# Two more units' outputs brought to features by TensorE, ScalarE for a first step, and a new written order

## The chip, the cores and the metric

The kernel runs on one core of one Trainium2 chip. The time is device microseconds of one execution; before, it is the median of three runs. A profiled execution gives a trace: for each engine (TensorE or PE, VectorE or DVE, ScalarE or ACT, GpSimd or POOL, and SyncE or SP, which issues DMAs) each instruction with its start and duration.

## The reference

A gated linear attention, one state matrix per batch and head, followed by a gated MLP. q, k, v and alpha are float32; the three weights are float64, which the kernel reads as pairs of 32-bit words.

```python
for t in range(S):                                  # B, H, S, D = 4, 8, 768, 48
    state = alpha[:, :, t, :, None] * state + einsum('bhd,bhe->bhde', k[:, :, t], v[:, :, t])
    y[:, :, t] = einsum('bhd,bhde->bhe', q[:, :, t], state)
x = y.transpose(0, 2, 1, 3).reshape(B * S, H * D)   # 3072 tokens, 384 features
g = x @ w_gate                                      # 384 -> 1536
return (g * sigmoid(g) * (x @ w_val)) @ w_out       # 1536 -> 384
```

## The kernel before, in words

**Attention.** The 768 steps of a batch are cut into four units of 192 steps, so there are 16 units, u = 0 to 15. Per unit: alpha, k and q are loaded (words La, Lk, Lq of the written order) and turned so that channels lie on partitions. For units 0 to 3 TensorE turns them (L394): a copy first spreads the rows (pa, pk, pq, L382), then T transposes them into PSUM, and ea, ek, cq copy them out (L798). For the later units VectorE transposes (tr, tk, tq, L374). Two scans on VectorE build the decay products (G, L439, and f, L448; z is a small memset behind f). mk multiplies k by them (L824 or L827), q does it for q (L465 or L467), and qc copies a part of that. k's rows are needed too: by TensorE's transposes (K, L492, copied out by kc, L496/L497) for units 0 to 3, by VectorE's (kr, L508) for the others. S are the scores on TensorE (L533), ma the causal mask on VectorE (L567). B (L557; Bw for units 0 to 3) are the states' updates, ad (L581 to L590) adds them up, de (L596) decays the state into the next unit, V loads the values (L413) and vc copies some of them. Y are the unit's outputs (L612 to L629), yh and yl split them into a high and a low part (L643, L647).

**To features.** The MLP wants the outputs with features on partitions, in the tile xT. For units 0 and 1 TensorE does it with selecting matrices (R, two matmuls a word, L669), and x copies the result out of PSUM (L673). For the other units SP issues ten DMAs a unit (xr, L686).

**MLP.** 3072 tokens are eight blocks of 384; d_ff is twelve slices f of 128. A step s is a block and a slice. Per step: product g (nine matmuls, high and low parts, L702), silu on ScalarE (sl, L710), product v (L702), their product h on VectorE (L714), its high part hh on ScalarE (L718) and low part hl on POOL or VectorE (L723), and nine matmuls o of the output (L734), summed over f in PSUM. Steps 0 to 6 are block 0 with f 0 to 6, steps 7 to 13 block 1 with the same, steps 14 to 18 block 0 with f 7 to 11, steps 19 to 23 block 1 with them; from step 24 on whole blocks follow. Each of the products g and v has one PSUM bank, so the next g waits for sl, the next v for h. ot copies a finished block out (L746), os stores it (L751).

**Weights.** 36 pieces in 20 groups: w0 to w2 and w19 hold one piece, the others two (in the order g0, v0, then g, v of slice f and o of slice f-1). wl loads a group's words (L277, L280), three steps v0, v1, v2 cut a float32 out of two words (L148, L151, L154, VectorE), a makes the high part (L321) and p the low part (L325). A group's words lie where the next group's result will lie. A range check of all weights (wr loads again, wc checks, L296 and L297, ScalarE) and of alpha (Lc, ck) runs in the later part; a flag at the end decides whether a general path runs instead, which never runs here.

**Order.** The program is written as one string, ORDER, of 1520 words engine:name@banks. Each engine runs its own words in that sequence (t TensorE, v VectorE, s ScalarE, g POOL, y SP); between engines only semaphores hold things back. The setting-up (memsets, ident, sel) stands outside the string, and the framework places it between the words. Before, the string began like this for TensorE, up to product v12, and for VectorE, up to h0:

```
t: Ta0 Ta1 Tq0 Tk0 Tk1 Tq1 S0 K0.0 K0.2 K0.1 Ta2 Bw0 K1.2 K1.1 K1.0 S1 Ta3 Y0 Bw1 Tk2 R0.2 Y1 Tq2 R0.1 K2.1 R0.0 K2.0
   K2.2 Tk3 R1.1 R1.2 R1.0 S2 Bw2 Tq3 Y2 g0 K3.1 v0 g1 S3 K3.2 K3.0 v1 o0 Bw3 g2 v2 Y3 g3 v3 o1 g4 v4 g5 o2 o3 v5 o4 g6
   v6 g7 v7 o5 g8 o6 v8 g9 v9 g10 o7 o8 v10 g11 o9 v11 g12 v12
v: w0v0 w0v1 w0v2 w1v0 w1v1 w1v2 G0 w1p f0 q0 mk0 G1 f1 ma0.2 w2v0 w2v1 w2v2 ma0.0 ma0.1 w3v0 w3v1 w3v2 de1 G2 f2 yl0.0
   ma1.0 ma1.2 yl0.1 ma1.1 mk2 w2p w4v0 w5v0 w5v1 w6v0 w4v1 w4v2 yl1.1 x0.0 yl1.0 de2 w6v1 w6v2 G3 ma2.2 mk3 ma2.1 ma2.0
   w7v0 w7v1 w7v2 de3 f3 yl2.0 yl2.1 h0
y: La0 wl0 wl1 Lq1 La1 Lq0 Lk0 V1 Lk1 La2 Lk2 V0 Lq2 La3 wl2 wl3 Lk3 wl4 ... wl17 xr2 wl18 V4 V5 xr3 La4 La5 Lq4 ...
```

Of the kernel before, what the change touches and what calls it, by code (L numbers as in the profile page):

```python
# [43 lines left out]
y:La0 y:wl0 y:wl1 y:Lq1 y:La1 y:Lq0 y:Lk0 s:pa0 y:V1 t:Ta0@01 v:w0v0 v:w0v1 s:ea0 v:w0v2 v:w1v0 v:w1v1 s:w0a v:w1v2  # L44
v:G0 s:w1a y:Lk1 s:pa1 y:La2 s:pq0 t:Ta1@01 v:w1p y:Lk2 t:Tq0@23 v:f0 g:z0 s:pk0 y:V0 t:Tk0@45 s:pq1 v:q0 g:pk1 g:w0p
v:mk0 t:Tk1@23 s:ea1 y:Lq2 s:ek1 t:Tq1@45 v:G1 y:La3 t:S0@01 y:wl2 s:qc0 y:wl3 t:K0.0@2 s:pa2 t:K0.2@3 v:f1 g:z1
s:kc0.0 t:K0.1@6 y:Lk3 s:vc0 y:wl4 s:kc0.1 y:wl5 v:ma0.2 g:mk1 s:kc0.2 t:Ta2@26 s:pa3 y:wl6 t:Bw0@1 v:w2v0 s:cq1
v:w2v1 y:wl7 v:w2v2 g:q1 t:K1.2@3 v:ma0.0 s:ad0.1 t:K1.1@4 t:K1.0@5 v:ma0.1 s:kc1.2 y:wl8 s:kc1.1 v:w3v0 s:qc1 t:S1@34
# [5 lines left out]
t:Bw2@6 s:x1.1 y:wl14 s:x1.0 s:pq3 v:ma2.2 g:qc2 y:Lk4 v:mk3 t:Tq3@13 g:w4p s:ad2.0 s:ad2.1 v:ma2.1 v:ma2.0 v:w7v0
s:ad2.2 v:w7v1 y:wl15 t:Y2@02 v:w7v2 s:cq3 v:de3 s:w7a y:wl16 t:g0 v:f3 g:z3 s:yh2.0 s:yh2.1 s:vc3 t:K3.1@1 t:v0
y:wl17 s:sl0 v:yl2.0 g:q3 s:kc3.1 v:yl2.1 t:g1 y:xr2 v:h0 s:hh0 v:w7p s:qc3 t:S3@01 v:w5v2 s:sl1 t:K3.2@2 v:ma3.2
g:hl0 t:K3.0@3 s:w5a t:v1 v:ma3.1 s:kc3.0 v:ma3.0 s:w6a v:w5p t:o0 s:kc3.2 v:w8v0 v:w6p t:Bw3@0 v:h1 v:w9v0 s:hh1
v:w10v0 y:wl18 t:g2 v:w10v1 s:ad3.0 s:ad3.1 v:w8v1 y:V4 t:v2 s:sl2 v:w8v2 v:w9v1 s:w8a t:Y3@01 v:w9v2 t:g3 v:w8p s:w9a
y:V5 s:yh3.0 v:w11v0 s:yh3.1 v:h2 g:hl1 v:yl3.0 t:v3 s:hh2 g:w9p v:yl3.1 s:sl3 v:tk4 t:o1 y:xr3 g:hl2 v:h3 t:g4 s:hh3
v:w12v0 s:vc4 v:hl3 v:w12v1 t:v4 s:sl4 v:w12v2 t:g5 v:h4 v:w11v1 t:o2 s:sl5 v:w11v2 y:La4 v:w10v2 s:w12a t:o3 s:hh4  # L60
v:w12p y:La5 s:w10a t:v5 v:hl4 s:w11a v:w10p t:o4 v:w13v0 v:w13v1 t:g6 v:w13v2 v:h5 g:w11p s:w13a t:v6 s:sl6 v:tr4
s:hh5 g:hl5 t:g7 v:h6 y:Lq4 v:w14v0 s:hh6 t:v7 v:w15v0 s:sl7 v:w15v1 t:o5 v:w13p v:h7 g:hl6 t:g8 s:hh7 v:w14v1 t:o6
v:w14v2 s:sl8 v:w15v2 s:w14a t:v8 s:ot6.0 v:w16v0 s:ot6.1 y:os6.0 v:w16v1 y:os6.1 t:g9 v:h8 g:hl7 s:hh8 v:w16v2 t:v9
s:sl9 v:hl8 s:w16a v:G4 t:g10 s:ot6.2 y:os6.2 t:o7 v:f4 g:z4 s:sl10 t:o8 v:h9 g:mk4 t:v10 s:hh9 g:hl9 v:tq4 t:g11
g:w15a v:h10 y:Lk5 t:o9 s:sl11 g:w15p v:kr4.0 s:hh10 v:kr4.1 t:v11 g:hl10 v:kr4.3 t:g12 g:q4 v:h11 v:kr4.2 s:hh11
t:v12 s:sl12 g:hl11 s:qc4 v:tr5 t:S4@01 g:w16p t:B4@2 v:h12 y:Lq5 v:ma4.2 g:w14p t:o10 v:tk5 s:ad4.0 v:ma4.1 t:o11
y:La6 s:hh12 v:ad4.1 g:hl12 v:ma4.0 t:g13 v:ad4.2 v:w17v0 t:o12 s:sl13 v:w17v1 y:wl19 v:w18v0 t:v13 v:w18v1 v:w18v2
t:Y4@01 v:h13 v:w17v2 s:hh13 t:g14 s:yh4.0 y:V6 v:G5 s:w17a s:yh4.1 t:v14 s:sl14 v:de5 s:vc5 v:yl4.1 g:hl13 t:g15
# [1038 lines left out]
```

## Time and profile before

| what | value |
|---|---|
| median of three runs | 576.37 us (576.31 to 577.98) |
| the profiled execution: its own time | 574.98 us |
| its span, first to last instruction | 573.2 us |
| TensorE busy | 546.3 us, 95% |
| VectorE busy | 385.0 us, 67% |
| ScalarE busy | 248.4 us, 43% |
| POOL busy | 147.0 us, 26% |
| granted TensorE clock, mean | 0.989 |

Times are read from the start of the span. The "idle before" of a group or a row is the engine's idle time just ahead of it, with what ended it. A row of the timeline gives start, length, engine, line, operation and tiles, and how many instructions are merged. Busy shares are averages over stretches that are limited by different things, so the prediction reads them by stretch.

### The profile page before, as it was taken

How to read it: one execution, taken by the hardware profiler on the slowest of the kernel's cores; microseconds unless marked ns; L12 is line 12 of the kernel's file. 1: busy time of each engine (PE TensorE's matmuls, PEld its weight loads, DVE VectorE, ACT ScalarE, POOL GpSimd, SP SyncE). 2: the span in 40 equal slices, each digit the busy share in tenths (PEclk: the TensorE clock that was granted, in tenths of full speed). 3: DMA queues.
4: the chain of work that ended last, by engine and by line, in shares of the span. 5: the costliest groups of instructions: out<-in, count | busy, mean ns of one | idle time of the engine just before them, and what ended most of it. 6: DMA issues, size and time to landing. Idle time of an engine off the chain costs nothing.

```text
span 573.2 us, 13708 instructions
## 1 busy us (share of the span) xinstructions
PE 546.3 (95%) x5510; PEld 527.2 (92%) x5510; DVE 385.0 (67%) x596; ACT 248.4 (43%) x573; POOL 147.0 (26%) x169
## 2 busy tenths in 40 slices
PE   4797998999999999999999999999999999999995
PEld 3576988999999999999999999999999999999995
DVE  7699998899999998899877297894872221111111
ACT  5867543324221222223154555543365556656222
POOL 6232322274325323115330012032120010112210
PEclk9978999999999999999999999999999999999999
DMA  8898956143366544546677665633844452321001
GB/s 238 270 307 250 247 125 145 43 115 81 86 147 164 136 117 107 124 91 145 170 169 191 172 181 132 179 110 102 207 125 123 128 151 63 94 76 59 0 1 47
DMA packets 95366, 77.65 MB, mean 135 GB/s; under 512 B 32832, under 2 KB 92224, under 8 KB 95296
## 3 DMA queue, kind: packets, MB, share of 16 engines
q1 hardware_dynamic: 95152, 76.51, 50.0%
q8 instruction: 45, 0.74, 0.6%
q14 instruction: 25, 0.20, 0.1%
q10 hardware_dynamic: 144, 0.20, 0.1%
HBM read 62.52 MB, written 5.90 MB: 119 GB/s over the span
## 4 chain that ended last, share of the span: by engine, by line
PE 88%; DVE 4%; ACT 2%; SPq 2%; issue 1%; DMA 1%; DVEq 0%; ACTq 0%
PE v L702 26%; PE ops L734 26%; PE g L702 25%; PE A L557 3%; PE y L629 2%; PE s L533 2%; PE pt L394 1%; SPq L686 1%; PE y L612 1%; PE y L613 1%; DVE t L154 1%; DVE t L151 1%; DMA raw<-in_moe_w_val_dram 1%; DVE w L325 1%; PE s L557 1%
## 5 line engine op out<-in xcount | busy, mean ns | idle before, releaser
L702 PE MATMUL v<-xT,w 128*128 128x384 f32 x864 | 167.6, 338 | 3.3 <-DVE h L714 3.3
L702 PE MATMUL g<-xT,w 128*128 128x384 f32 x864 | 166.9, 337 | 0.0
L734 PE MATMUL ops<-w,hh 128*128 128x384 f32 x576 | 158.8, 337 | 0.0
L702 PEld LDWEIGHTS v<-xT,w 128*128 128x128 f32 x864 | 150.5, 188 | 5.2 <-DVE h L714 4.4
L702 PEld LDWEIGHTS g<-xT,w 128*128 128x128 f32 x864 | 150.9, 188 | 0.6
L723 POOL TENSOR_TENSOR hl<-h,hh 128x384 fp32r<-128x384 f32 x67 | 70.5, 1052 | 250.3 <-ACT hh L718 236.0
L714 DVE TENSOR_TENSOR h<-h,v 128x384 f32<-128x384 f32 x96 | 53.0, 552 | 119.0 <-PE v L702 106.6
L718 ACT CAST hh<-h 128x384 fp32r<-128x384 f32 x96 | 49.0, 512 | 150.9 <-DVE h L714 77.5
L734 PEld LDWEIGHTS ops<-w,hh 128*128 128x128 f32 x576 | 105.3, 188 | 0.9 <-ACT K L497 0.2
L734 PE MATMUL ops<-w,hl 128*128 128x384 f32 x288 | 96.7, 336 | 0.0
L710 ACT ACTIVATE h<-g 128x384 f32<-128x384 f32 x96 | 47.0, 490 | 114.1 <-PE g L702 102.9
L508 DVE STREAM_TRANSPOSE K<-Gs 32x384 f32<-32x384 f32 x96 | 54.7, 570 | 5.4 <-PE A L557 3.8
L734 PEld LDWEIGHTS ops<-w,hl 128*128 128x128 f32 x288 | 54.1, 188 | 0.0
L567 DVE TENSOR_TENSOR X<-s,mask 64x384 f32<-64x384 f32 (+1 forms) x48 | 26.0, 550 | 5.8 <-DMA wc<-in_moe_w_out_dram 3.4
L439 DVE TENSOR_TENSOR_SCAN Gs<-AT,inj 128x772 f32<-128x772 f32 x16 | 29.0, 1814 | 1.1 <-ACT AT L798 0.8
L448 DVE TENSOR_TENSOR_SCAN AT<-AT,back 128x771 f32<-128x771 f32 x16 | 29.2, 1824 | 0.7
L723 DVE TENSOR_TENSOR hl<-h,hh 128x384 fp32r<-128x384 f32 x29 | 16.1, 557 | 16.3 <-ACT hh L718 16.2
L394 PE MATMUL pt<-ident,wide 128*128 128x128 f32 x72 | 14.2, 352 | 13.1 <-ACT wide L382 8.2
L394 PEld LDWEIGHTS pt<-ident,wide 128*128 128x128 f32 x72 | 10.7, 181 | 15.4 <-POOL sel L348 5.1
L452 POOL MEMSET AT<- 128x3 f32 x16 | 1.7, 106 | 89.1 <-DVE AT L448 89.1
L297 ACT ACTIVATE wc<-wc,wbias 128x384 f32<-128x384 f32 x36 | 23.3, 647 | 1.2
L325 POOL TENSOR_TENSOR w<-t,w 128x768 fp32r<-128x768 f32 (+1 forms) x11 | 19.1, 1744 | 15.3 <-ACT w L321 15.0
(113 smaller groups left out, 606.2 us busy)
## 6 DMA issues: line engine op xcount, KB each, us to landing
xT<-X SPq DMA_DIRECT2D x84, 72.0 KB, 2.2
raw<-in_moe_w_gate_dram SPq DMA_DIRECT2D x12, 384.0 KB, 8.0
raw<-in_moe_w_val_dram SPq DMA_DIRECT2D x12, 384.0 KB, 7.8
V<-in_v_dram SPq DMA_DIRECT2D x96, 48.0 KB, 2.5
raw<-in_moe_w_out_dram SPq DMA_DIRECT2D x12, 384.0 KB, 7.8
wc<-in_moe_w_gate_dram SPq DMA_DIRECT2D x12, 384.0 KB, 5.0
wc<-in_moe_w_val_dram SPq DMA_DIRECT2D x12, 384.0 KB, 3.7
wc<-in_moe_w_out_dram SPq DMA_DIRECT2D x12, 384.0 KB, 3.9
```

Of the source, the lines that this page charges most:

```text
L325: eng.tensor_tensor(out=lo, in0=src, in1=hi.bitcast(F32), op=ALU.subtract)
L394: nc.tensor.transpose(pt[:, j - js.start, :], Wd.rearrange("p j e c -> p (j e c)")[:, j * P : (j + 1) * P], ident)
L439: nc.vector.tensor_tensor_scan(*(x.rearrange("p g t -> p (g t)")[:, ::-1] for x in (Gs, AT, inj)), 0.0, op0=ALU.mult, op1=ALU.add)
L448: nc.vector.tensor_tensor_scan(Af, Af, back[:, 1 : n + 1], back[:, 0:1], op0=ALU.mult, op1=ALU.add)
L508: nc.vector.transpose(out=bass.AP(k0.tensor, k0.offset, [k0.ap[0], (G * 2 * D, NU), (2 * D, G), (1, 32)]), in_=Kg[j * BO + x : j * BO + x ...
L567: nc.vector.tensor_tensor(out=X[r, z, f * GF : (f + 1) * GF, :].rearrange("r g (c t) -> r g c t", c=NU), in0=sps[f][r].rearrange("r g (c t ...
L702: nc.tensor.matmul(pt, wsp[kind, f][a][:, kt * P : (kt + 1) * P], xT[blk][:, b_, kt, :], start=(n == 0), stop=(n == 3 * KT - 1),)
L710: nc.scalar.activation(h, acc.pop(("g", blk, f)), AF.Silu)
L714: nc.vector.tensor_tensor(out=h, in0=h, in1=acc.pop(("v", blk, f)), op=ALU.mult)
L718: nc.scalar.copy(out=hh, in_=acc["h", blk, f])
L723: eng.tensor_tensor(out=hl, in0=acc.pop(("h", blk, f)), in1=hh.bitcast(F32), op=ALU.subtract)
L734: nc.tensor.matmul(ops[blk][i], h[b_][:, i * P : (i + 1) * P], wsp["o", f][a], start=(first and n == 0), stop=(last and n == 2),)
```

## The change

- R2 and R3 are new: TensorE brings the outputs of units 2 and 3 to features (six words of two matmuls, six copies x2, x3 on ScalarE), and xr2 and xr3 (twenty DMAs on SP) are gone. Their outputs lie in regions of weight groups 15 and 16 meanwhile, as those of units 0 and 1 lie in 18 and 17.
- The cut of a weight's words may begin on ScalarE. Its first step is then another one: it scales the low word down to its top three bits; the second step, on VectorE, shifts the high word and joins it; the third sets the upper bits. Begun on VectorE, it is the same three steps with the second and the third exchanged. The new order begins 17 groups on ScalarE (all but w2, w4 and w19).
- The cut relies on a narrower range of the weights, and wc tests it with a third operation on ScalarE per piece (a shift and an absolute value before the last one).
- The order is a new one of 1534 words. k's rows of units 8 and 10 are TensorE's (K, kc) and no longer VectorE's (kr); V0 is loaded from ScalarE's queue, first of all its words; the first spreading (pa0) is POOL's; q0's transposed rows are copied out by ScalarE first (cq0), q2's no longer are; the last store (os95.2) is SP's, no longer ScalarE's; 25 hl go from POOL to VectorE and 16 the other way; ten z, seven q and five mk go to VectorE. An eighth PSUM bank, held before by a tile that nothing used, can be named.

```diff
-    busy32 = inj[:, 0, 0:P]
-    busy = busy32.bitcast(BF16)
...
-    return [ lambda: nc.vector.tensor_scalar(...), lambda: ..., lambda: ... ]
+    def first(eng):
+        by.append(eng)
+        if eng is nc.scalar:
+            eng.activation(t, lo, AF.Copy, scale=LOW3)
+        else:
+            eng.tensor_scalar(
+                out=t, in0=hi, scalar1=3, scalar2=0xC0000001, op0=ALU.logical_shift_left, op1=ALU.bitwise_or
+            )
+    def second(eng):
+        if by[0] is nc.scalar:
+            eng.scalar_tensor_tensor(out=t, in0=hi, scalar=3, in1=t, op0=ALU.logical_shift_left, op1=ALU.bitwise_or)
+        else:
+            eng.scalar_tensor_tensor(out=t, in0=lo, scalar=29, in1=t, op0=ALU.logical_shift_right, op1=ALU.bitwise_or)
+    def third(eng):
+        eng.scalar_tensor_tensor(out=t, in0=hi, scalar=0x3FFFFFFF, in1=t, op0=ALU.bitwise_or, op1=ALU.bitwise_and)
...
         nc.scalar.activation(dev, dev, AF.Abs, accum_out=wviol[:, 1, i : i + 1])
-        nc.scalar.activation(dev, dev, AF.Relu, bias=wbias, scale=-1.0, accum_out=wviol[:, 0, i : i + 1])
+        nc.scalar.activation(dev, dev, AF.Abs, bias=wbias[:, 0:1])
+        nc.scalar.activation(dev, dev, AF.Relu, bias=wbias[:, 1:2], accum_out=wviol[:, 0, i : i + 1])
...
-            st["Y"] = st["X"] if u >= UPB else p2.tile(
-                [112, 2, G, T], F32R, tag=f"w{len(wgroups) - 2 - u}", name=f"Y{u}", bufs=1
+            st["Y"] = st["X"] if u >= RU else p2.tile(
+                [112, 2, G, T], F32R, tag=f"w{len(wgroups) - 2 - (u if u < UPB else 2 * UPB + 1 - u)}", name=f"Y{u}", bufs=1
...
-    BANKS = ("A0", "A1", "A2", "ops0", "ops1", "vps", "gps")
+    BANKS = ("A0", "A1", "A2", "ops0", "ops1", "vps", "gps", "ops2")
```

The new order, TensorE up to v12, VectorE up to h12, and the first words of the others:

```
t: Ta0 Ta1 Tq0 Tk0 K0.0 K0.2 K0.1 Tk1 Tq1 S0 Bw0 K1.0 Ta2 K1.1 K1.2 S1 Y0 Ta3 Bw1 R0.0 R0.2 Tk2 R0.1 Y1 Tq2 K2.2 K2.0
   K2.1 R1.2 R1.0 Tk3 R1.1 S2 g0 Tq3 K3.2 K3.1 K3.0 v0 g1 Bw2 S3 v1 g2 v2 Y2 o0 o1 R2.1 R2.2 g3 v3 o2 R2.0 Bw3 g4 v4 o3
   Y3 g5 v5 g6 o4 v6 R3.0 R3.1 R3.2 o5 g7 v7 g8 v8 g9 o6 S4 B4 v9 g10 v10 g11 o7 o8 v11 o9 g12 Y4 o10 v12
v: G0 w0v1 f0 z0 w1v1 q0 w0v2 mk0 G1 f1 mk1 w2v0 w2v1 w2v2 ma0.2 ma0.0 ma0.1 z1 w0p w1v2 de1 w3v1 G2 f2 w1p yl0.0 yl0.1
   ma1.2 w4v0 w3v2 ma1.1 ma1.0 mk2 w4v1 w4v2 yl1.0 yl1.1 q2 w4p x1.0 w2p G3 mk3 w6v1 w6v2 de2 w5v1 w5v2 f3 w6p ma2.0
   ma2.1 ma2.2 h0 tk4 ma3.2 hl0 h1 w8v1 w9v1 w9v2 h2 ma3.0 w8v2 yl2.0 yl2.1 de3 w9p hl2 w7v1 w7v2 z3 tr4 ma3.1 h3 w7p hl3
   G4 w11v1 w11v2 w10v1 w10v2 h4 w12v1 kr4.1 yl3.1 kr4.2 h5 kr4.3 yl3.0 tq4 kr4.0 h6 w14v1 w13v1 w13v2 w12v2 w14v2 hl6 h7
   w12p f4 q4 tk5 h8 ma4.2 w15v1 ad4.1 h9 tr5 ma4.1 w15v2 w16v1 ad4.2 h10 ma4.0 hl9 w16v2 G5 w18v1 h11 w18v2 w17v1 w17v2
   mk5 kr5.1 h12
s: V0 pa1 ea0 vc0 w0v0 pq0 w1v0 cq0 pk0 ea1 pk1 pq1 kc0.0 kc0.1 ek1 kc0.2 qc0 pa2 cq1 ad0.1 ad0.2 w3v0 ea2 w1a kc1.1 qc1
   ad0.0 pa3 w2a kc1.0 kc1.2 yh0.0 yh0.1 ad1.0 ad1.1 x0.2 ad1.2 pq2 x0.1 x0.0 yh1.0 yh1.1 ...
g: pa0 w0a q1 z2 pk2 vc1 w3a w3p w4a pk3 vc2 q3 w5p hl1 w9a w8p mk4 w10p hl4 ...
y: Lq1 La0 La1 wl0 Lq0 wl1 Lk0 Lk2 La2 Lk1 V1 wl2 wl3 wl4 wl5 La3 wl6 wl7 wl8 Lk3 wl9 Lq2 wl10 wl11 wl12 Lq3 V2 La4 V3
   Lk4 wl13 La5 V4 Lq4 wl14 V5 Lk5 wl15 ...
```

More of the change, by code (lines that the diff above doesn't have):

```diff
@@ L43 @@
 ORDER = """
[L44 to L48, printed above, removed]
@@ L54 @@
[L54 to L58, printed above, removed]
@@ L59 @@
[L59 to L68, printed above, removed]
@@ L330, in weight_group, with cut @@
         t = []
-        def cut(i):
+        def cut(i, eng):
             if not i:
                 t.append(p2.tile([P, size], U32, tag="t", name=f"t{n}", bufs=NTS))
-            single(nc, raw, t[0])[i]()
+                t.extend(single(nc, raw, t[0]))
+            t[1 + i](eng)
         return (
-            [lambda i=i: cut(i) for i in range(3)],
+            [lambda eng, i=i: cut(i, eng) for i in range(3)],
             [lambda eng: high(eng, t[0].bitcast(F32))],
```

209 lines of the change are left out of this document (112 added, 97 removed).

## The prediction

> **What bounds the kernel now.** I read the page first: the chain of work that ended last is mostly TensorE (PE).
>
> ```profile
> PE 88%; DVE 4%; ACT 2%; SPq 2%; issue 1%; DMA 1%; DVEq 0%; ACTq 0%
> ```
>
> An average hides where. So I asked for the busy time in five stretches, cut at the first product g0 (56.2), at product v1 (63.1), at the end of product v12 (122.62) and at the last matmul:
>
> ```profile
> 0.00:56.20 56.20, 39.31 (x768) 33.01 (x768) 46.17 (x71) 38.14 (x87) 20.64 (x40) 0.91 0.88 264
> 56.20:63.10 6.90, 6.90 (x90) 6.50 (x88) 6.06 (x8) 4.56 (x11) 3.32 (x5) 1.00 1.10 258
> 63.10:122.62 59.52, 56.25 (x424) 54.13 (x424) 53.42 (x68) 23.75 (x46) 19.60 (x17) 1.00 0.45 121
> 122.62:566.45 443.83, 443.82 (x4238) 433.60 (x4238) 279.30 (x452) 181.45 (x429) 103.41 (x108) 1.00 0.46 120
> 566.45:573.20 6.75, 0.00 (x0) 0.00 (x0) 0.00 (x0) 0.48 (x1) 0.00 (x0) 0.79 0.27 96
> ```
>
> The columns are length, then PE, weight loads, VectorE (DVE), ScalarE (ACT), GpSimd (POOL), then granted clock and DMA. From 122.62 to 566.45 PE is never idle: there only PE work counts, and each matmul added costs its full time. In front of that PE is idle 16.9 us before g0 and 3.27 us between v1 and v12. So the change can win only in the first 123 us, and it pays for whatever PE work it adds. In those 123 us the full engine is VectorE. Its own windows end with hidden step h0 and with h12:
>
> ```profile
> 5.30:60.69 55.39, 47.11 (x69) 0.91 0.94 274
> 60.69:123.41 62.72, 56.62 (x70) 1.00 0.47 125
> ```
>
> It is idle 8.3 us in the first and 6.1 us in the second. The timeline names the larger waits:
>
> ```profile
> 5.35 0.36 DVE L148 TENSOR_SCALAR t<-raw 128x384 uint32<-128x384 uint32 x1 [1.29 <-DMA raw<-in_moe_w_gate_dram]
> ...
> 15.54 1.77 DVE L439 TENSOR_TENSOR_SCAN Gs<-AT,inj 128x772 f32<-128x772 f32 x1 [0.85 <-ACT AT L798]
> ...
> 23.67 0.59 DVE L148 TENSOR_SCALAR t<-raw 128x384 uint32<-128x384 uint32 x1 [3.84 <-DMA raw<-in_moe_w_gate_dram]
> ...
> 60.13 0.56 DVE L714 TENSOR_TENSOR h<-h,v 128x384 f32<-128x384 f32 x1 [0.76 <-PE v L702]
> ...
> 95.25 1.58 DVE L374 STREAM_TRANSPOSE AT<-L 128x768 f32<-128x768 f32 x1 [2.44 <-POOL hl L723]
> ```
>
> The last one is put down to POOL, but the chain of waits goes from this transpose to the landing of alpha's rows (La4; the last row below is the chain's), and those are issued on SP's queue behind both repacks:
>
> ```profile
> 12.13 3.90 SPq L413 DMA_DIRECT2D V<-in_v_dram  x6
> ...
> 17.51 0.59 SPq L280 DMA_DIRECT2D raw<-in_moe_w_gate_dram  x1
> ...
> 63.59 9.35 SPq L686 DMA_DIRECT2D xT<-X  x10
> ...
> 82.92 7.32 SPq L686 DMA_DIRECT2D xT<-X  x10
> ...
> 91.87 3.25 DMA L<-in_alpha_dram
> ```
>
> **The change, part by part.** Prices of the operations:
>
> ```profile
> L374 DVE STREAM_TRANSPOSE trk<-L 128x768 f32<-128x768 f32 x12 | 19.6, 1630 | 1.8 <-DMA L<-in_k_dram 1.8
> ...
> L439 DVE TENSOR_TENSOR_SCAN Gs<-AT,inj 128x772 f32<-128x772 f32 x16 | 29.0, 1814 | 1.1 <-ACT AT L798 0.8
> ...
> L154 DVE SCALAR_TENSOR_TENSOR t<-raw,t 128x768 uint32<-128x768 uint32 x16 | 18.1, 1144 | 0.4
> ...
> L647 DVE TENSOR_TENSOR X<-y,X 112x384 fp32r<-112x384 f32 x28 | 14.8, 553 | 8.6 <-ACT X L643 8.5
> ...
> L321 ACT CAST w<-t 128x768 fp32r<-128x768 f32 x14 | 11.6, 832 | 11.9 <-DVE t L154 11.9
> ...
> L148 DVE TENSOR_SCALAR t<-raw 128x768 uint32<-128x768 uint32 x16 | 10.2, 654 | 0.8 <-POOL w L325 0.8
> L596 DVE SCALAR_TENSOR_TENSOR V<-SE,Gs 48x192 f32<-48x192 f32 x24 | 9.6, 401 | 0.5
> ...
> L325 DVE TENSOR_TENSOR w<-t,w 128x768 fp32r<-128x768 f32 x7 | 6.7, 952 | 0.1
> ...
> L467 DVE TENSOR_TENSOR X<-trq,AT 112x768 f32<-112x768 f32 x4 | 3.8, 956 | 0.1
> ```
>
> *Start to v1.* In the new order h0 lets v1 start, as now, and VectorE's queue up to h0 changes so. First steps of weights 0 and 1 go to ScalarE (half width, about 0.35 each), those of 3, 5, 6 with 0.654 each; weight 7's three steps come later (0.65 and about 2.2); weight 5's third step comes in (1.1). Subtractions w0p, w4p, w6p come in (0.5 + 2 x 0.95), as do q2 and mk1 (0.96 each); de3 (2 x 0.4) and yl2 (2 x 0.55) go behind h0. Two memsets of z are 0.1. Sum: -0.7 - 2.0 - 0.65 - 2.2 + 1.1 + 2.4 + 1.9 - 0.8 - 1.1 + 0.1 = -1.9, so 45.2 us of work.
>
> When does it start? The first scan (G0) now heads VectorE's queue and waits for ScalarE, whose queue begins with V0's six DMA issues. Rows of three engines' timelines that bear on it:
>
> ```profile
> 4.29 0.67 ACT L382 COPY wide<-Le 128x576 f32<-128x576 f32 x1 [2.19 <-DMA Le<-in_alpha_dram]
> ...
> 6.27 0.20 ACT L208 ACTIVATE first<-one 1x1 f32<-1x1 f32 x1
> 6.38 0.95 ACT L798 COPY AT<-pt 128x384 f32<-128x384 f32 x2
> ...
> 1.98 1.18 DVE L204 MEMSET V<- 128x1344 f32 x1 [0.23 <-issue]
> ...
> 6.57 2.03 POOL L351 CAST sel<-ident 48x48 fp32r<-48x48 f32 x4
> ```
>
> They wait for the memset of that tile (3.2) and take 3.9 by SP's row; the page's ScalarE queue issues nothing of the kind, so between 0 (nearest: hidden behind alpha's landing) and 3.9. I take 3.9, the same DMA. A widening (0.67) and alpha's two copies (0.95) follow: G0 at 8.8 to 8.9. If pa0, now POOL's, stands behind POOL's set-up casts (end 8.6), it is about 11.8; but on ScalarE pa0 (4.29) ran ahead of the set-up's own first activation (6.27), so I take 8.9 and keep +2.9 for the range.
>
> Waits: of the 8.3 us now, 1.3 stand ahead of the first weights (row 5.35), where nothing waits any more with G0 in front, and I count none of them. The 3.84 go: without V0 on SP, and with two loads moved back, the third weights' DMA is issued near 11 instead of 17.51, long before w2v0 (about 21). The 0.85 goes, since three steps now lie between the first pair of scans and G1; the 0.76 too, since v0 is done far ahead of h0. What is late next is ScalarE, which also gets cq0 (two copies): by my following of its queue it has 0 to 1 us to spare at each step. Left: 1.5. So h0 ends at 8.9 + 45.2 + 1.5 = 55.6, and v1 starts at 55.7 instead of 63.1. Of PE's work ahead of v1 only Y2 has moved behind it.
>
> *v1 to v12.* PE's prices at full clock:
>
> ```profile
> 40.35 0.60 PE L669 MATMUL xp<-Y,sel 112*128 112x384 f32 x2
> ...
> 62.38 0.96 PE L492 MATMUL kps<-ident,Gs 112*64 112x112 f32 x8
> ...
> 122.55 0.93 PE L533 MATMUL s<-X,Gs 48*64 48x64 f32 x48
> ...
> 124.47 0.44 PE L734 MATMUL ops<-w,hh 128*128 128x384 f32 x1
> ...
> 127.70 1.72 PE L702 MATMUL g<-xT,w 128*128 128x384 f32 x9
> ...
> 132.48 0.27 PE L612 MATMUL y<-X,V 128*64 128x64 f32 x1
> ...
> 134.17 0.44 PE L702 MATMUL g<-xT,w 128*128 128x384 f32 x1
> ```
>
> By starts: S and B of a unit 1.92, two products after them 3.23 (1.6 each, some 0.1 of it for the switch between kinds), Y 1.69, eight K transposes 0.72 (to 63.10). An R step, two matmuls, is not seen undisturbed: between two products' matmuls (2 x 0.17) and 0.60; I take 0.43. New in this stretch: Y2 and Y4 (3.4), S4 and B4 (1.9), one more o product (1.6), R2 and R3 (six, 2.6), six more switches (0.6): 10.1. PE's work is 56.25 + 10.1 = 66.4.
>
> VectorE's, h0 to h12, grows too: in come one transpose (1.63), a scan (1.81), seven half tiles (3.9), q4 and mk5 (1.9), de3 and two ad4 (eight small ones of 0.4 at most, 2.6) and a kr (at most 1.6): 13.4. Out go four subtractions (3.8), and the cuts change by five of 1.1 in and nine first steps of 0.654 out (-0.4). That is +9.2: 65.8 us beside PE's 66.4, with both fuller than now. The repacks' 16.7 us leave SP, La4 is issued right behind V2, and the wait of 2.44 with PE's gaps behind it (about 2 of the 3.27) goes. I leave PE 1.3 us idle: 67.7. v12 ends at 55.7 + 67.7 = 123.4. The six evacuations x2, x3 (and twelve copies for K8 and K10 later, each at most 0.83) are ScalarE's, 40% busy here (23.75 of 59.52).
>
> *v12 to the end.* Moved ahead: 1.92 + 1.69 + 1.6 = 5.2. Added: K8 and K10 as TensorE transposes, six words at 0.36 (2.2), and eight more switches (0.8); they spare VectorE eight kr steps, worth nothing where PE never waits. So 443.83 - 5.2 + 3.0 = 441.6. All other PE work is the same. The third operation of each weight check is on ScalarE: at most 36 x 0.83 = 30 us beside 181 of 444 busy, hidden by PE; without that cover it would stand in front of silus.
>
> *Tail.* Today's 6.75 has the last store on ScalarE's queue; now it follows two on SP: between 0 and one issue (0.65); 0.4.
>
> Sum: 123.4 + 441.6 + 7.15 = 572.15 against 573.2, so 1.05 less. The profiled execution took 574.98, 1.4 under the median of 576.37; the difference is put on the median: **575.3**. About 0.3% (1.7 us) can be told from no change, so this is a "same": won are 7.4 us ahead of v1, less Y2's 1.7, and 2.0 of gaps, together 7.7; the added PE work (R 2.6, K 2.2, switches 1.4) takes 6.2 of it and the tail 0.4.
>
> **The rivals.** *Faster.* VectorE keeps only 0.5 us of waits before h0, and PE none between v1 and v12: 1.0 + 1.3 less, 573.0. For it: every step that I followed was ready before VectorE came to it, and PE already runs 444 us without a gap. Against it: ready by under 1 us each time.
>
> *Slower: VectorE becomes the limit between h0 and h12.* If it keeps the 6.1 us of idle it has there today, its stretch is 65.8 + 6.1 = 71.9 instead of PE's 67.7: +4.2, 579.5. It decides (over 0.3% slower, 1.7 + 1.05 above the forecast) from 67.7 - 65.8 + 2.8 = 4.7 us of idle. For it: an engine in order that meets PE, ScalarE and POOL at each step; against: 2.44 of the 6.1 was alpha's.
>
> [...]
>
> *Checks late.* ScalarE's longer checks stand before silus: if a third of the 20 us (36 x 0.55, L647's size) showed, +6.6: 581.9. Against it: 40% busy there.
>
> **How the numbers follow.** Forecast 0.30, colder start 0.08 (both within 0.3%: 0.38), faster 0.36, slower 0.26 (VectorE 0.21, checks 0.05). The likeliest single outcome's own range is 574.6 to 578.1. The range to hold 8 in 10 reaches into both sides: from 572.0 (the faster case with V0's issues hidden by 1 us) to 579.8 (VectorE's case, or pa0 late, +2.9).
>
> **What would show it.** Right: no wait of VectorE for the third weights, v1 near 55.7, v12's end near 123.4, no PE gap behind it, 441.6 to the last matmul. Wrong: h0 past 58 with ScalarE as releaser (start), VectorE idle over 4.7 us from h0 to h12 (the rival), PE gaps after v12, or R and K words dearer than 0.43 and 0.36.

## The result, and the profile after

The changed kernel took 581.61 us (median of six runs, 580.50 to 584.29) and the kernel before 577.17 on the same chip (six runs, 576.01 to 578.50): a ratio of 1.0081, 95% interval 1.0058 to 1.0104. It is slower, by 0.8%; forecast were 575.3 and no change. The profiled execution of after has a span of 581.3 and an own time of 583.07, 1.5 over its median, while that of before (574.98) is 2.2 under its six runs' median: the two traces differ by 8.1, the medians by 4.4, and runs of one kernel by about 1% (the 23 of before beside e1_v0_sp: 573.68 to 580.11). So terms are read from traces here, and verdicts from medians.

The chain of work that ended last, in the page of after, has more DMA and VectorE and less TensorE than before:

```profile
PE 84%; DVE 7%; DMA 4%; ACT 2%; issue 1%; POOL 0%; SPq 0%; ACTq 0%; DVEq 0%
```

The busy time of after in the prediction's five stretches, cut at g0, v1, the end of v12 and the last matmul (same columns as before):

```profile
0.00:53.35 53.35, 33.28 (x594) 29.11 (x594) 36.07 (x57) 31.35 (x74) 17.21 (x41) 0.94 0.88 264
53.35:65.22 11.87, 10.07 (x194) 9.59 (x190) 11.57 (x17) 8.91 (x20) 3.45 (x3) 1.00 0.57 145
65.22:132.77 67.55, 66.70 (x681) 64.59 (x679) 65.19 (x83) 36.68 (x69) 32.62 (x26) 0.97 0.45 122
132.77:574.30 441.53, 440.89 (x4086) 430.31 (x4085) 272.43 (x440) 204.87 (x470) 76.00 (x83) 1.00 0.46 117
574.30:581.30 7.00, 0.00 (x0) 0.00 (x0) 0.00 (x0) 0.48 (x1) 0.00 (x0) 0.75 0.27 92
```

And VectorE's two windows, to the ends of h0 and h12:

```profile
5.30:64.74 59.44, 44.45 (x65) 0.94 0.86 254
64.74:133.75 69.01, 66.62 (x86) 0.98 0.44 120
```

| term | predicted | after |
|---|---|---|
| first scan G0 starts | 8.9 | 12.24 |
| VectorE's work from G0 to h0 | 45.2 | 44.45 |
| VectorE's idle time between them | 1.5 | 8.05 |
| h0 ends / v1 starts | 55.6 / 55.7 | 64.74 / 65.22 |
| v1 to the end of v12 | 67.7 | 67.55 |
| then to the last matmul | 441.6 | 441.53 |
| tail | 7.15 | 7.00 |
| span | 572.15 | 581.3 |

(64.74 - 12.24 - 44.45 = 8.05.) All from v1 on came within 0.2 of the forecast (how much of that is luck is said below). The miss is 6.3 in the medians (581.61 against 575.3) and 9.15 in the traces (581.3 against 572.15), and 9.5 of it lie ahead of v1. ScalarE's timeline in after shows where it begins (ACTq are its DMA issues):

```profile
3.20 0.71 ACTq L437 DMA_DIRECT2D V<-in_v_dram  x1
...
4.00 1.32 ACTq L437 DMA_DIRECT2D V<-in_v_dram  x2
...
6.78 3.82 ACTq L437 DMA_DIRECT2D V<-in_v_dram  x3
10.64 0.67 ACT L406 COPY wide<-Le 128x576 f32<-128x576 f32 x1 [5.21 <-DMA V<-in_v_dram]
11.22 0.98 ACT L811 COPY AT<-pt 128x384 f32<-128x384 f32 x2
...
14.50 0.43 ACT L503 COPY U<-V 64x288 f32<-64x288 f32 x1 [1.84 <-DMA V<-in_v_dram]
14.96 0.54 ACT L158 ACTIVATE t<-raw 128x384 uint32<-128x384 uint32 x1
```

V0's six issues hold ScalarE from 3.20 to 10.60, 7.4 us where SP's row gave 3.9, so pa1 and ea0, and with them G0, stand behind 10.6. A single issue still takes 0.6 to 0.7 (3.82 for three is mostly waiting between them), and SP's own issues are spread out in the same time, one every 1.0 to 3.0 us from 5.10 on (its timeline in after):

```profile
5.10 0.60 SPq L447 DMA_DIRECT2D Le<-in_k_dram  x1
8.13 0.60 SPq L447 DMA_DIRECT2D L<-in_k_dram  x1
9.18 0.60 SPq L447 DMA_DIRECT2D L<-in_alpha_dram  x1
10.67 0.60 SPq L447 DMA_DIRECT2D L<-in_k_dram  x1
```

The DMA engines are full then; the stretch from 5 to 10 us of after:

```profile
5.00:10.00 5.00, 1.54 (x6) 1.14 (x6) 0.00 (x0) 0.42 (x2) 2.45 (x9) 1.00 1.04 303
```

Full engines alone are not the reason: before, with a share of 1.07 in the same stretch, V1's six issues took SP only 3.93.

```profile
5.42 3.93 SPq L413 DMA_DIRECT2D V<-in_v_dram  x6
```

What the issues wait for can be read from the landings in after. With both queues counted together, each of the seven issues from 5.10 to 10.67 starts 0.02 behind the landing of the DMA eight issues before it, and in the traces of before (516 DMAs) and of after (496) never more than eight of the program's DMAs are under way at once. V0's first issue is the 5th of all and lands at 8.39; the 13th, V0's fifth, starts at 8.41. Its second, the 7th of all, lands at 9.98; the 15th, V0's last, starts at 10.00. The chain of waits of after has this step, and the landing of that last issue behind it:

```profile
4.00 5.98 DMA V<-in_v_dram
10.00 4.40 DMA V<-in_v_dram
```

Then, in ScalarE's timeline above, vc0's second copy, put ahead of the first weight step w0v0, waits 1.84 for V0's landing. VectorE's timeline in after shows both, and two waits for TensorE later:

```profile
12.24 1.77 DVE L463 TENSOR_TENSOR_SCAN Gs<-AT,inj 128x772 f32<-128x772 f32 x1 [8.18 <-ACT AT L811]
15.53 0.56 DVE L166 SCALAR_TENSOR_TENSOR t<-raw,t 128x384 uint32<-128x384 uint32 x1 [1.52 <-ACT t L158]
...
42.32 1.12 DVE L591 TENSOR_TENSOR X<-s,mask 64x384 f32<-64x384 f32 x2 [2.42 <-PE s L581]
45.48 1.04 DVE L837 TENSOR_TENSOR Gs<-pt,Gs 128x384 f32<-128x384 f32 x2 [2.04 <-PE pt L418]
```

TensorE, in turn, stalls without a releaser inside two words, S1 and Bw1 (its timeline in after):

```profile
32.69 0.81 PE L557 MATMUL s<-X,Gs 48*64 48x64 f32 x39 [1.78 <-issue]
...
39.49 1.75 PE L581 MATMUL A<-V,K 128*48 128x48 f32 x37 [2.22 <-issue]
```

### The profile page after: what moved, and what is told of

The parts are those of the page before. It is cut to its first block, busy times and chain, and to the rows that moved or that the text cites. A ratio compares the mean times of both kernels' runs of the same rounds, so it can differ in the third digit from the quotient of the medians.

```text
span 581.3 us, 13772 instructions
## 1 busy us (share of the span) xinstructions
PE 550.9 (95%) x5546; PEld 533.6 (92%) x5546; DVE 385.3 (66%) x594; ACT 282.3 (49%) x631; POOL 129.3 (22%) x151
## 4 chain that ended last, share of the span: by engine, by line
PE 84%; DVE 7%; DMA 4%; ACT 2%; issue 1%; POOL 0%; SPq 0%; ACTq 0%; DVEq 0%
PE v L726 25%; PE ops L758 24%; PE g L726 24%; DMA V<-in_v_dram 3%; PE A L581 2%; PE s L557 2%; PE y L653 2%; DVE t L176 1%; DVE t L166 1%; DMA raw<-in_moe_w_val_dram 1%; PE kps L516 1%; PE y L636 1%; PE y L637 1%; DVE AT L472 1%; PE pt L418 1%
## 5 line engine op out<-in xcount | busy, mean ns | idle before, releaser
L747 POOL TENSOR_TENSOR hl<-h,hh 128x384 fp32r<-128x384 f32 x58 | 65.1, 1123 | 275.5 <-ACT hh L742 273.6
L532 DVE STREAM_TRANSPOSE K<-Gs 32x384 f32<-32x384 f32 x80 | 45.6, 570 | 1.5
L747 DVE TENSOR_TENSOR hl<-h,hh 128x384 fp32r<-128x384 f32 x38 | 21.1, 556 | 25.3 <-ACT hh L742 25.0
L472 DVE TENSOR_TENSOR_SCAN AT<-AT,back 128x771 f32<-128x771 f32 x16 | 33.0, 2065 | 0.6
L581 PE MATMUL A<-V,K 64*48 64x48 f32 (+1 forms) x720 | 22.8, 213 | 2.2 <-issue 2.2
L319 ACT ACTIVATE wc<-wc,wbias 128x384 f32<-128x384 f32 x36 | 23.4, 651 | 1.2
L320 ACT ACTIVATE wc<-wc,wbias 128x384 f32<-128x384 f32 x36 | 23.4, 649 | 1.2
```

Source lines behind the costliest of these rows:

```text
L472: nc.vector.tensor_tensor_scan(Af, Af, back[:, 1 : n + 1], back[:, 0:1], op0=ALU.mult, op1=ALU.add)
L532: nc.vector.transpose(out=bass.AP(k0.tensor, k0.offset, [k0.ap[0], (G * 2 * D, NU), (2 * D, G), (1, 32)]), in_=Kg[j * BO + x : j * BO + x ...
L581: nc.tensor.matmul(to[j * BO : j * BO + D, g - gs.start, :], Ks[r, x, g, KC[j]], Vd[r, x, g, VC[j]], start=(x == 0 or not whole), stop=(x ...
L747: eng.tensor_tensor(out=hl, in0=acc.pop(("h", blk, f)), in1=hh.bitcast(F32), op=ALU.subtract)
```

## The experiments

**Theory:** the start was lost by V0 at the head of ScalarE's queue and vc0 ahead of w0v0; the rest is as predicted. **Rivals:** A, TensorE's stalls and its half clock; B, ScalarE is too slow with the first weight steps; besides, VectorE's limit, and the checks. Each run has its own runs of the kernel before beside it, so the ratios to it are compared; one of 0.001 is 0.58 us.

**V0 on SP** (e1_v0_sp), V0's place undone, and vc0's with it:

```diff
 y:La1
-s:V0
 y:wl0 ... s:ea0 y:La2
-s:vc0
 y:Lk1 v:G0 y:V1
+y:V0
 ... s:ek1
+s:vc0
```

> The changed kernel with one thing undone: unit 0's values (V0) are issued by SP behind V1 instead of first on ScalarE's queue, and vc0 stands behind ek1 on ScalarE. Theory (the start is lost by V0's six issues at the head of ScalarE's queue and by vc0 ahead of the first weight step): G0 begins at 8.0 to 9.5 instead of 12.24, w0v1 waits under 0.5 instead of 1.52, and v1 begins at 58 to 61 instead of 65.2; the time is 4 to 6.5 under the changed kernel's, ratio to the kernel before 0.997 to 1.001. Rival A (TensorE's own stalls without a releaser and the half clock behind them decide): G0 is earlier, but v1 is earlier by under 1.5, ratio 1.005 to 1.008. Rival B (ScalarE is too slow with the first weight steps): as A, with VectorE waiting for ScalarE between G1 and h0.

Measured: 578.24, ratio 1.0024 (1.0001 to 1.0046). VectorE at the start of this kernel:

```profile
8.64 1.77 DVE L463 TENSOR_TENSOR_SCAN Gs<-AT,inj 128x772 f32<-128x772 f32 x1 [4.59 <-ACT AT L811]
10.32 0.53 DVE L166 SCALAR_TENSOR_TENSOR t<-raw,t 128x384 uint32<-128x384 uint32 x1
...
37.51 1.12 DVE L591 TENSOR_TENSOR X<-s,mask 64x384 f32<-64x384 f32 x2 [2.35 <-PE s L581]
40.25 1.02 DVE L837 TENSOR_TENSOR Gs<-pt,Gs 128x384 f32<-128x384 f32 x2 [1.62 <-PE pt L418]
```

G0 begins at 8.64 (predicted 8.9), the wait at w0v1 is gone, and 3.4 us of the median are back. v1 begins at 61.46 and the ratio is 1.0024, both a bit past the theory's 58 to 61 and 0.997 to 1.001, and far from rival A's: the places of V0 and vc0 are 3.8 of the 9.5, and two waits for TensorE stay.

**V0 late on ScalarE** (e1b_v0_late): as before, but `s:V0` behind `s:w1v0`.

> The changed kernel with V0 still on ScalarE's queue, but behind weight 1's first step instead of at the head, and vc0 behind ek1. If only the place at the head costs: the same as with V0 on SP, within 1 us. If six issues on ScalarE's queue cost ScalarE 7.4 us wherever they stand (3.20 to 10.60 in the changed kernel): G0 at 8.0 to 9.5, but cq0, pk0 and ea1 behind the issues are late by 4 to 7, VectorE waits for ea1 (G1) or ek, and v1 stays past 62, ratio 1.003 to 1.008.

Measured: 581.61, ratio 1.0086 (1.0053 to 1.0120), v1 at 64.39: nothing is won. The second reading holds. ScalarE and VectorE of this kernel:

```profile
11.41 5.79 ACTq L437 DMA_DIRECT2D V<-in_v_dram  x6
17.24 0.99 ACT L811 COPY trq<-pt 128x384 f32<-128x384 f32 x2 [6.10 <-DMA V<-in_v_dram]
```
```profile
8.83 1.77 DVE L463 TENSOR_TENSOR_SCAN Gs<-AT,inj 128x772 f32<-128x772 f32 x1 [4.78 <-ACT AT L811]
...
18.27 0.96 DVE L491 TENSOR_TENSOR X<-trq,AT 112x768 f32<-112x768 f32 x1 [4.60 <-ACT trq L811]
```

G0 is early, but six issues cost ScalarE 5.8 here and VectorE waits 4.60 at q0 instead. It isn't the place at the head that costs but issues on a queue whose engine VectorE waits for: the six that took SP 3.90 before took ScalarE 5.8 here and 7.4 in after.

**One part alone, on the kernel before** (e2_before_v0_act): `s:V0` as the first word, `s:pa0` made `g:pa0`.

> The kernel before with one part of the change alone: V0 first on ScalarE's queue, and the widening pa0 on POOL. VectorE there starts with the first two weights, which do not wait for ScalarE. Theory (issues at the head of ScalarE's queue take it to 10.6): ea0 about 11, G0 about 11.8 to 12.3 instead of 8.43, h0 and v1 later by 2 to 4, and the third weights' wait (3.84 of VectorE) goes since SP is free of V0, which gives some back: ratio 1.000 to 1.006. Rivals A and B (the head of ScalarE's queue is not what costs): v1 as before or up to 3.8 earlier, ratio 0.993 to 1.000.

Measured: 577.50, ratio 1.0020 (0.9996 to 1.0044). G0 begins at 12.94 instead of 8.43, and VectorE's wait for the third weights is 0.9 instead of 3.84: part of what the issues take, SP's free queue gives back. The ratio lies in the theory's range; no change at all lies just inside the interval. In the trace v1 begins at 68.50 instead of 63.10, later by more than the theory's 2 to 4. That execution took 579.39, 1.9 over the median of its kernel, and the one of before lies 2.0 under the median of the runs beside it (576.95), so how much of the 5.4 is the change and how much the spread stays open.

**K words back to VectorE** (e3_kr): K8, kc8, K10 and kc10 out, eight kr of VectorE in.

```diff
-t:K8.1@2 s:kc8.1 t:K8.2@0 t:K8.0@1 s:kc8.2 s:kc8.0     (and the six of unit 10)
 v:tq8
+v:kr8.0 v:kr8.1
 ...
+v:kr8.2 v:kr8.3
 v:q8
+v:kr10.0 v:kr10.1 behind yl9.0, v:kr10.2 v:kr10.3 behind tr11
```

> The changed kernel with the K words of units 8 and 10 taken back to VectorE's kr steps (eight kr for six K and six kc). Theory (TensorE never waits there, so its added work costs its full time): start as in the changed kernel, the stretch from v12 to the last matmul shorter by 2.2 + 0.8 = 3.0, ratio to the changed kernel 0.995, to the kernel before 1.003. Rival (TensorE has slack there, or VectorE is late with kr): within 0.7 of the changed kernel, with idle of TensorE in that stretch.

Measured: 583.20, ratio 1.0116 (1.0083 to 1.0149). The theory's step falls. From the end of v12 to the last matmul, and TensorE's waits there, in this kernel:

```profile
131.17:575.10 443.93, 439.19 (x4062) 428.41 (x4061) 281.29 (x456) 201.25 (x458) 76.05 (x83) 1.00 0.45 117
```
```profile
PE ops L758 <- DVE part L766: 1.6, 1, 1.6
PE v L726 <- DVE h L738: 1.6, 2, 1.2
PE s L557 <- DVE X L491: 1.5, 1, 1.5
```

The K words cost 1.70 of TensorE's time (440.89 - 439.19), not 3.0; and with the kr where I put them VectorE is late four times, and TensorE idle 4.74. So "worth nothing" doesn't hold for these places: TensorE doesn't wait because VectorE was relieved. Other places for the kr were not tried, and 1.0116 is not clear of the change's 1.0081.

**R words back to SP** (e4_xr): R2, R3 and their x words out, `y:xr2` ahead of wl14, `y:xr3` ahead of wl15, Y2 and Y3 stored as before.

> The changed kernel with units 2 and 3 brought to features by SP's DMAs again, ten a unit (ahead of wl14 and wl15), their outputs lying where they did before, in place of the six R words and their evacuations. Theory (the R words cost TensorE their full time, 2.6 and some switches, since it waits only 0.85 between v1 and v12; but VectorE, idle 2.4 there, and alpha's rows behind 16.7 us of issues on SP take it back): v1 to v12 between 64.5 and 68.5, time within 2 of the changed kernel's. By the prediction's own price (R costs 2.6 and spares a wait of 2.0 to 2.4): 0.2 to 1.2 under the changed kernel. Rival (SP's repacks are what the change was rid of): v1 to v12 over 70, the time 3 or more over the changed kernel's.

Measured: 590.77, ratio 1.0233 (1.0207 to 1.0258); v1 to v12 takes 74.05. TensorE's waits in that stretch of this kernel:

```profile
PE g L725 <- DMA xT<-X: 5.3, 3, 3.3
```

The rival holds: in this order, the features of block 1 come too late through SP. What the R words cost TensorE by themselves can't be read beside these waits; what they are worth is 9 us and not 2, with the DMAs in these places.

**First steps back to VectorE** (e5_dve_first): every `s:wNv0` made `v:wNv0`, just ahead of `v:wNv1`.

> The changed kernel with all 17 first steps of the weights' conversion taken back from ScalarE to VectorE, each just ahead of its second step. Theory (ScalarE's first steps were not what made the start late, and VectorE, busy 66.6 of 69.0 between h0 and h12, has no room): ahead of h0 VectorE has 2 x 0.36 + 3 x 0.65 = 2.7 more and loses the wait of 1.52 for ScalarE; behind it twelve steps of 0.65 are 7.8 more, of which at most 2.4 fit into its idle time: h0 to h12 takes 73 to 75, and the time is 5 to 8 over the changed kernel's, ratio to the kernel before 1.017 to 1.022. Rival B (ScalarE too slow with the first steps makes the start late): v1 begins 2 to 4 earlier than 65.2, and the total is the changed kernel's within 2.

Measured: 591.87, ratio 1.0244 (1.0217 to 1.0271), past the theory's 5 to 8. Rival B falls: v1 begins at 66.04. VectorE from h0 to h12 in this kernel (PE, weight loads, VectorE):

```profile
64.92:144.54 79.62, 73.68 (x741) 68.45 (x734) 76.14 (x97) 28.31 (x60) 33.61 (x26) 0.97 0.39 104
```

76.14 of 79.62 is busy: this is the slower rival of the prediction, VectorE as the limit, which the first steps on ScalarE keep away.

**Two operations a check** (e6_two_ops): L319 out, L320 as before.

> The changed kernel with the range check of the weights in two operations a piece, as before, so it leaves out the upper limit that the third operation tests. Theory (the third operation lies on ScalarE beside TensorE's work, 36 of about 0.55 beside 441 us): the time is that of the changed kernel within 0.6, ratio to the kernel before 1.006 to 1.010. Rival (checks late: they stand in front of silus): 2 to 6.6 under the changed kernel.

Measured: 581.52, ratio 1.0075 (1.0046 to 1.0103), that of the change. The third operation (group of after) is hidden, as far as 0.3% can be told:

```profile
L320 ACT ACTIVATE wc<-wc,wbias 128x384 f32<-128x384 f32 x36 | 23.4, 649 | 1.2
```

**The other 5.8 us (9.52 - 3.76): three tries at the loads.** With V0 on SP, TensorE still stalls (1.59 and 1.24) and VectorE still waits for it (2.35 and 1.62), while the DMA engines are full (share 1.08 from 25 to 45 us). In the first try (e8_spread) the loads wl8 to wl12 went behind Lq3 and V2.

> The changed kernel with V0 on SP, as in the run before with that name, and now with ten of the weight loads (wl8 to wl12) issued behind Lq3 and V2 instead of ahead of them: between 25 and 45 us the DMA engines, busy all the time there (share 1.08), get free time, and no load comes later than its use. Theory of TensorE's own stalls (1.59 ahead of S1's 39 matmuls and 1.24 in Bw1, with no releaser shown, come while the DMA engines are full, since TensorE's instructions come by DMA too): the two stalls fall under 0.4 each, the half clock behind them (0.50 from 30 to 40) is shorter, VectorE's waits of 2.35 and 1.62 go or halve, v1 begins at 57 to 59.5 instead of 61.46, and the time is 2 to 4 under that of V0 on SP alone: ratio to the kernel before 0.995 to 0.999. Rival (the stalls have another cause): stalls and half clock as they are, v1 within 1 of 61.5, ratio 1.001 to 1.004.

Measured: 585.86, ratio 1.0130 (1.0101 to 1.0160), and it tells nothing of the loads: moving V2 put it ahead of the word Y0, so that unit 0's outputs were made from unit 2's values, and Y0 waited 10.3 for their landing. The second (e9_spread2) moves weight loads alone: wl5 behind Lk3, wl6 ahead of Lq3, wl7 to wl12 behind V2.

> V0 on SP as in e1_v0_sp, and the weight loads wl5 to wl12 moved back on SP's queue (wl5 behind Lk3, wl6 ahead of Lq3, wl7 to wl12 behind V2), each still ahead of its use; nothing else moves, the values' loads least of all. The DMA engines should be free from about 25 to 40. Theory (TensorE's stalls without a releaser, 1.59 ahead of S1's last 39 matmuls and 1.24 in Bw1, are its instructions, 16 KB at a time over a DMA queue of their own, coming late behind weights): both under 0.5, the half clock from 29.4 to 39.6 shortened or gone, VectorE's waits of 2.35 and 1.62 halved, v1 at 57 to 59.5 instead of 61.46, ratio to the kernel before 0.994 to 1.000. Rival (they come at that rate with free DMA engines too, as words of many small matmuls use them up): stalls of 1.0 to 1.8 and the half clock stay, v1 within 1 of 61.5, ratio 1.001 to 1.004.

Measured: 583.81, ratio 1.0109 (1.0078 to 1.0141). S1's stall is 0.44, and v1 begins at 59.92, 1.5 earlier; but V3 and unit 4's k rows now stand behind the weights on SP, and right after h0 VectorE loses more than was won (its waits, 59 to 80):

```profile
DVE trk L398 <- DMA L<-in_k_dram: 6.2, 1, 6.2
```

The third (e12_spread3) mends that:

```diff
 y:Lk3
+y:wl5
 ...
+y:wl6
 y:Lq3 ... y:V2
+y:wl7 y:wl8 y:wl9
 ... y:La4 ... y:Lk4
+y:V3 y:wl10 y:wl11 y:wl12
```

> V0 on SP, and the weight loads moved back once more, now with the alpha and k rows of unit 4 ahead of V3 and of wl10 to wl12 on SP's queue, so that Lk4 lands before h0 ends. In e9_spread2 the loads' move made v1 begin 1.5 earlier (59.92, S1's stall 0.44 instead of 1.59), and VectorE then waited 6.19 for Lk4. Theory (the loads' pressure on DMA makes part of TensorE's stalls, and the loss of e9_spread2 was Lk4's alone): v1 at 59.5 to 60.5, VectorE's wait for Lk4 under 0.5, v1 to v12 67.5 to 68.5, 1 to 2 under e1_v0_sp: ratio to the kernel before 0.998 to 1.001. Rival (e9_spread2 lost by the late weights, not by Lk4): v1 to v12 over 70 with waits for weights, ratio over 1.005.

Measured: 574.37 (nine runs), ratio 0.9961 (0.9938 to 0.9984): faster than both kernels, than the one before by 0.4%, and better than expected. Its stretches up to the last matmul, cut as above, and VectorE's largest waits from 15 to 60 us:

```profile
0.00:46.92 46.92, 30.91 (x595) 27.22 (x595) 36.09 (x57) 31.30 (x74) 16.65 (x41) 0.93 0.78 233
46.92:58.79 11.87, 10.06 (x194) 9.59 (x190) 11.57 (x17) 8.89 (x20) 3.46 (x3) 1.00 0.66 140
58.79:125.23 66.44, 65.39 (x682) 63.00 (x680) 65.07 (x83) 36.26 (x69) 33.13 (x26) 1.00 0.61 172
125.23:566.98 441.75, 440.75 (x4086) 430.23 (x4085) 271.81 (x440) 204.93 (x470) 75.90 (x83) 1.00 0.45 117
```
```profile
DVE X L591 <- PE s L581: 1.2, 1, 1.2
DVE Gs L837 <- PE pt L418: 1.0, 1, 1.0
```

v1 begins at 58.79, 6.4 earlier than in after; the two waits fell from 2.35 and 1.62 to 1.2 and 1.0. The stalls are not what went, though: in S1 1.51 us are left, in Bw1 1.04. So the second half of the theory holds (e9_spread2 lost by Lk4) and the first falls. What is shorter around these words is the half clock: 3.4 us (33.8 to 37.2) instead of 10.2 (29.4 to 39.6), with 3.4 more at 16.7 (clock 0.67 from 15 to 20), well ahead of them. That the moved loads made it so is not shown, and e14_all below, at a clock of 1.00 from 30 to 40 and with its v1 at 59.20, is no faster.

**The loads without V0** (e15_loads): the same moves on SP, V0 first on ScalarE as in the change.

> The changed kernel with V0 first on ScalarE's queue as in the change, and only the weight loads wl5 to wl12, V3 and Lk4 moved on SP's queue as in e12_spread3. Theory (two separate losses of the new start): 3 to 4.5 under the changed kernel, ratio to the kernel before 1.000 to 1.003, with G0 still past 12. Rival (the loads matter only once the start is early, since VectorE has slack behind a late G0): within 1 of the changed kernel, ratio 1.006 to 1.010.

Measured: 581.09, ratio 1.0071 (1.0048 to 1.0095): the rival holds. The two losses don't add: V0's place alone brings 0.6%, both 1.2%, and the loads alone 0.1%, which is inside the noise, although v1 begins 1.9 earlier in this trace (63.35).

**S3 behind v1, and Tk2 earlier.** With V0 on SP, v1 starts 1.1 after h0, since S3 ahead of it waits 2.02 for POOL. e10_s3 moves `t:S3` behind `t:v1`; e11_both does so beside e9_spread2's loads.

> V0 on SP as in e1_v0_sp, and the scores S3 moved behind product v1 on TensorE. In e1_v0_sp S3 waits 2.02 for q3, which POOL multiplies until then, and v1 stands behind it, 1.1 after h0. Theory: v1 follows h0 within 0.1 and S3 fills later time, so 0.7 to 1.3 are won: ratio to the kernel before 1.000 to 1.002. Rival (ma3 and VectorE behind S3 are then late, and TensorE waits for h1 or h2 instead): within 0.4 of e1_v0_sp.

> V0 on SP, the weight loads moved back as in e9_spread2 and S3 behind v1. Theory: both gains add up: 3 to 5 under e1_v0_sp, ratio to the kernel before 0.992 to 0.998, which would be faster than both kernels. Rival (neither stalls nor S3 set the end): ratio 1.000 to 1.004.

Measured: 580.71, ratio 1.0047 (1.0028 to 1.0067), and 583.85, ratio 1.0117 (1.0086 to 1.0148). In the first v1 follows h0 within 0.1, as said, but no time is won: VectorE waits 2.7 for unit 4's k rows in its place. The second inherits e9_spread2's loss. e13_tk2 moves `t:Tk2` ahead of R0.0, e14_all does so beside e12_spread3's loads.

> V0 on SP as in e1_v0_sp, and the transposes Tk2 ahead of R0.0 and R0.2 on TensorE instead of behind them (R0.0 and R0.2 took 1.52 there at half clock). Theory (between mk0 and mk2 TensorE is the bound, not VectorE): VectorE's wait of 1.62 for Tk2 goes, and what is behind it comes up to 1.5 earlier: v1 0.7 to 1.6 earlier than 61.46, ratio to the kernel before 0.999 to 1.002. Rival (VectorE's queue or S3 and q3 on POOL set v1 anyway): v1 within 0.5 of 61.46, the wait coming back elsewhere.

> V0 on SP, the loads as in e12_spread3 and Tk2 as in e13_tk2. Theory: both add up, v1 at 58 to 59.5, 2 to 3.5 under e1_v0_sp: ratio to the kernel before 0.996 to 1.000. Rival: what the one gains the other already had; as the better of the two.

Measured: 578.79, ratio 1.0029 (1.0008 to 1.0051), and 575.77, ratio 0.9970 (0.9949 to 0.9992). In the first the wait for Tk2 fell to 0.67, and 2.24 came back at yl1, whose TensorE words now stand later; v1 begins at 62.13, 0.7 later than with V0 on SP alone. So the rival's second part, the wait coming back elsewhere, holds there, and the rival of the second run holds too: e12_spread3 stays the best.

## Why the prediction was wrong

**The step that failed** is "So h0 ends at 8.9 + 45.2 + 1.5 = 55.6". The work term was right (44.45). Two terms were not:

*G0 at 8.9.* I bounded V0's issues on ScalarE by 0 and 3.9, "the same DMA" by SP's row; they took 7.4 in after, 5.8 in e1b_v0_late. SP's row is of six issues that stand where the DMA eight before each has landed already (0.84 to 2.62 us earlier, in the trace of before), so it holds no waiting. At the head of ScalarE's queue V0's six are the 5th to the 15th of all DMAs, every other one, and the last three each wait 1.0 to 1.5 for a landing. With V0 off ScalarE's queue G0 began at 8.64 and vc0's wait was gone (e1_v0_sp): that is 3.8 of the 9.5 at v1.

*Waits of 1.5.* VectorE was idle 8.05. 1.52 is vc0's: I listed VectorE's and ScalarE's words, but did not ask what vc0, a copy of values, waits for. 2.42 and 2.04 are waits for TensorE between mk0 and mk2. I had treated VectorE as the full engine up to h0 and took TensorE's words there at the full clock; with stalls and a half clock TensorE is the later one. Both have a part, by two traces: in e6_two_ops, with the change's words and only 3.4 us of half clock there, the wait for Tk2 is 0.74 and the one behind Bw1's stall of 2.22 is still 2.42; in e15_loads, where neither word stalls, the two are 0.8 and 0.6. No run took the stalls alone away, so this half of the cause is read from traces. With the waits halved in e12_spread3, v1 is 2.7 earlier than with V0 on SP (58.79 against 61.46). There 3.1 are left up to the forecast, worked out from this kernel's G0 (9.09), work (44.46) and end of h0 (58.30): 3.2 more idle time (4.75 instead of 1.5), 0.2 from G0, 0.4 from S3, less 0.7 of work.

**What held, and by what luck.** v1 to v12 was to take 67.7 and took 67.55; the rest 441.6 and 441.53; the tail 7.15 and 7.00. The first two agree by luck in part. The 67.55 has 3.4 us of half clock in it (65.8 to 69.2, below), which the sum did not have; the same words take 66.55 without it (e6_two_ops), so the sum was about 1.1 too long. In the 441.6 TensorE's work was put 0.7 too high (441.6 against 440.89 busy: 1.3 too much for the K words, 0.6 too little elsewhere, where is not known), and 0.64 of idle time, put at nothing, made up for it. VectorE's work from h0 to h12 was to be 65.8 and was 66.62, with 2.4 of idle: under the 4.7 from which the slower rival decides. The checks are hidden (e6_two_ops). With V0 and the loads moved the change wins as was forecast: e12_spread3's ratio of 0.9961 lies near the forecast's 575.3 / 576.37 = 0.9981. Term by term it does not match: v1 is 3.1 later than forecast, and v1 to v12 (66.44) and the tail (6.32) are 1.3 and 0.8 shorter.

**Right sum, wrong reasons in it.** The K words cost 1.7 and not 3.0, and without them VectorE was late where its kr were put; the R words save more than 2. Each was priced as an addition to a kernel that had room for what it replaces. In the new order there was none.

**The colder start**, a longer time at half clock (chance 0.08), was not it. Half-clock stretches before and after, up to the last matmul:

```profile
27.60:34.40 6.80, 6.25 (x135) 5.55 (x135) 6.25 (x8) 4.77 (x11) 0.71 (x2) 0.50 1.08 366
44.70:48.10 3.40, 2.96 (x12) 2.95 (x12) 3.30 (x6) 2.57 (x8) 0.00 (x0) 0.50 0.46 72
```
```profile
38.50:45.30 6.80, 5.81 (x94) 5.63 (x95) 2.52 (x5) 1.39 (x4) 2.76 (x3) 0.50 1.03 301
65.80:69.20 3.40, 3.40 (x13) 3.40 (x12) 2.45 (x5) 2.88 (x7) 0.20 (x1) 0.50 0.51 130
```

Both have 10.2 us of it. But where it falls counts: before, VectorE was busy through it (6.25 of 6.80); in after it was busy 2.52 of 6.80 and waited. Even so v1 is no earlier in e6_two_ops, where 3.4 of these 6.8 us are at full clock: it begins at 65.73, with G0 0.6 later and a wait of 0.9 at yl1 in place of most of the one for Tk2.

## What to carry to other kernels

Here a DMA issue was work of the engine that issued it (0.6 to 0.7 us each on ScalarE and SP in after), and so was the time that it waited to be issued (7.4 for V0's six with their waits). It waited until the DMA eight issues back had landed: count how deep in the order of all queues an issue stands and when that landing comes, and see who waits for what is queued behind it. When VectorE's words are taken away from a stretch, follow the next engine through it at the clock that this stretch has. And price a replaced operation in the new order, not in the old one, where there was room for it.
